# A recorded order and its PSUM banks, replaced from the third transposed load on, in an LN + long convolution + gated MLP backward kernel

## The chip, the cores and the metric

The kernel runs on one core of a Trainium2 chip. The metric is the device time of one execution in microseconds (us). Before the change it is 425.65 us, the median of three runs (423.27 to 426.55).

## The reference, cut to what matters

The kernel returns the output and all nine gradients of a block on x of 2048 tokens by 512 channels, in bf16. With xn the layer norm of x:

```python
xn = _layernorm(x)
kv  = k_shift * v                                  # k_shift: 4-tap causal filter of k
y   = irfft(rfft(kv_pad) * rfft(ssm_k_pad))[:S] + kv * ssm_D
h   = (xn @ w_gate) * (xn @ w_up)                  # 1376 hidden channels
out = x + xn * y + h @ w_down
grads = vjp(out, (x, k, v, shift_k, ssm_k, ssm_D, w_gate, w_up, w_down))(grad_out)
```

The long convolution and its two gradients are done as Fourier transforms by matmul, in three stages that pass through DRAM.

## The kernel before, in words

Tokens are held as 16 rows r of 128 partitions. The work falls into four parts that overlap.

- A first part makes the layer norm, the hidden activations in six slices of the hidden width (mlp_rows, L416) and the weight gradients (dw_gen, L582). The hidden products go to the DRAM buffer HD.
- A second part (a_gen, s_gen) makes the first two stages of the Fourier transforms. Its result lies in the DRAM buffer CX.
- A turn (turn_gen, L615) transposes those slices of the hidden products that stay in SBUF: the last slice by TensorE in twelve groups of eight blocks with a ScalarE copy after each ("turn k", k being the first block), and rows 8 to 15 of the last but one by four transposing DMAs of two rows each ("turn load r").
- The last part is the one that the change touches. It runs over eight chunks n of two rows, rr = 0 and 1.

In the last part a chunk has these steps, named by their functions:

- **c_load(n)** (L676) brings 1.5 MB from CX into the one buffer C. It can be issued once the matmuls last_dft(n-1) have read C.
- **last_dft(n)** (L719), 24 small matmuls of 32 columns of weights into three two-bank PSUM slots; **c_dkv**, **c_y**, **c_o5** (L737, L729, L755) copy one slot each with ScalarE and go on with VectorE. c_o5 has one buffer and waits for its last store.
- **hd_load(n)** (L642) is a transposing DMA from HD into hdP[n % 2], 1152 rows of 768 for n up to 3 and 896 rows after. It can be issued once all matmuls of chunk n-2 have been done, and every matmul of chunk n waits for it.
- **y_o(n, rr)** (L784): 11 matmuls of 128x512 and a VectorE add into m[n % 2]; with rr = 1 the store of the output follows. **y_load(n)** (L688) refills m[n % 2] with x and so waits until the store of chunk n-2 has landed.
- **y_x(n, rr)** (L801): 22 matmuls of 128x512, then a VectorE and ScalarE chain for the gradient of x, with its store.
- **c_dsk(n)** (L764): VectorE products of the k gradient path and 8 small matmuls into one bank that is summed over all chunks; then **k_load** of the next rows.
- **dk_pair(r0)** (L710): seven VectorE operations into the one buffer dk, and its store. The next dk_pair begins by writing dk and so waits until the store has landed.
- **dkv_load** (L682) brings v and the shifted k for the next chunk.

All DMAs are issued by SyncE (SP) in one order, so an issue that waits holds all later ones. The functions above only record operations (class Eng, L143). emit (L181) decodes the string PLAN (L34): first a permutation of the 2271 recorded operations (a run of up to four matmuls is one), then a bank for each of the 398 PSUM slots. Each engine, and SP as the DMA queue, issues its operations in that order:

```python
    def emit(plan):
        raw = zlib.decompress(base64.b85decode(plan))
        order = struct.unpack(f"<{len(ops)}H", raw[:2 * len(ops)])
        for s, b in zip(slots, raw[2 * len(ops):], strict=True):
            s.base = Q[b // 2] if s.n == 2 else halves[b]
        ...
            for i in order:
                for fn in ops[i].fns:
                    fn()
```

A slot of two banks lies at an even bank ("F2" is banks 2 and 3, "h7" is bank 7). All instructions of the record carry line 173 in the profile (the line that calls the recorded function), so they are told apart by operation, shape, tiles and place in the order. big is the one SBUF tile, PP the one PSUM tile.

Of the kernel before, what the change touches and what calls it, by code (L numbers as in the profile page):

```python
# [17 lines left out]
S = 2048  # L18
D = 512
F = 1376  # L20
R = 16
# [9 lines left out]
RING = 28  # L31
RO = [0, 16, 24, 40, 56, 72]
EPS = 1e-5
PLAN = "c-l=@V-Ti0&yLfzZQHhO+qP}nwr$(CjpN;8V{!03yYHWGn(4G@t|V9PnWi^DCP)GdB_IW)gkq2Y1hPO$h!2S&As{4&;-FyQ5FiRfg=kO;qC*TQ4ap!Tl!aK32+BZv=m_N?HpGEk5Esfr1xN)OAs*z0`H%-TK?mprogp>khXT+7TEPNH3V9(76of9&8nQwmC=B^vEOdkJPy}j2S7-)Bp(Qkjy3hmaKu@R#)nF*hfcj7cszU>)3hAH`41<}_7%D*<m<Z#cG7N@>Fa&DAIA{XBpdw6z;V=Sf!eN*WXJ8fVf~GJE_P|J(0IOjVjE3FN7WzS2*bBX31>}S=FblF^R@?{sVK%IUBXAEAV;?vRN$?<4$D~*T=fWJA2g&dN9D;0E6W2h0SPOlj7G}qvU^1+O^{^NQz<c=-mcT&R01IIeY=zBm3${UeI0rw&QuqZjz!t~|7vN8bj>}*>{0iq`3S5L8a2&G13AhiJAO{|W-{2ZNf@AO)lH*B8fu|rP{th|uGNi)WkQ)Dh>mc|8d<tnWE#80!a1+wuT}Y3)Fau`9hmZ;Hz;nn9neip$#?RmrsEv70F)tdvfb8%uI06Q&gLM%xAGU*fSRda&evE<zupl<Tzn~%h2Zit|d=7;%DmKE#_!gc*5p06%uqm#`4Y(2CK?~f3e?v=bg{`p-ehJO+J+#H0unlA2XdHu2;45f{(Qq@i#}3#WzkrSy6Sv@DJc8pf7IwnU*af@d1nh=!@F+6Yg0JBf9K*lm8|aQ>@ik1w*q8&x;Xkk)dtwj#4!(t{I1MM_ah!v_a60zJt=I?WVqctsGq4{{!Uebk7vfAjfjjXe_QzQ`00-i39E4A42o1&+xC@71T%3o?a44?CB{&R+<5C<-gWwDn#rZe_pTTk*M$4fUjl_7k3K!#QY)y;sG&ZD!SPUCcacoQpFg~`S`ZS!@ViRghEvOmo!3J~+J5y6?NoTPOmB5*F9!uf{EQO`9BbC8(*oj6^J1UEpFcFr+D|j6VZ{STVkC*W(R=`_$8!O^$yn`cY6y3#2xR5I2J*<LN@gg>-`&bPh;6vPtG3fw4!pHaopJFU(PowY|&Z5{9hvL$6oJ}wAC0?R<^a*~7bLbH6$ItL{`~u@s0{RjYQX-m5U*SCJN2w?`<)Oi}4^vYbdWDJUHI||Nl$NexS(;B@<2P82^3pr$Kx61K<)iYHpDIu<DnQ@jclbSCfh3fU(o;psK$R#d{eVB>SjtG5=nDOW1?gwZOv$JaWudH8nSQ}v@i)vyzvCbHCuXO@l!N}l<Wz*J&>Or;Z?P!lq<7exM$<Jqi0|=l{0CFezxW>(qvBMRN)Qkd5mPl1nhI-B$;hcXrKCVLXaUuvC{&ViQB*2L(WoocqS{oNqEkJ(PK&7<-Jm+ugZj`CT1p#f8TF;^G>$gWc-leRXaG&1XEc$v(?D8Flju3^r1kWI*3o2oNgHSvZJ{YNjb_j-I!v2sDjlTLaD?{LCp4XQ(;@ni_Rs-3N-O9mI!1fxSGq|n={LGat7#Q2r=RH;Iz`{Z8Tyn?)93Vney6jvhEC99dPKs1&}a0JPSTSIN#%5$o|(U(44jc)Q6|pJU(uJ8g<n%v{)@KKZMsM2=nZA#?0lZ?P!7IJIr%;1;=d_3JAX~zQXU@4-_U*fj`A|__Y{|r<8chm$Hs4I7{8<8Je&We5j>Nl@xSs9jpTo%B9G#j9G^#XbdJJfxByS*Nt}SA@(iB9u{btY;>tXW=kP?X!U@^5AQ$4vJdUe!(0$|zI-V18Vvc+wox(}DFjwOr=szjKMVWOfFX8IEh>CGiu1hgURCN(Y(PX@olXG-U!O?U9AE)A6f=hB#jj0QHF~`t2nv!d9JnhVJwG^k)RGgYib9_ysHMtg-;aD15Q)?P7%jI|wrR4;gP|I^#t<4oUv8K~RnpE?19qz(Ov@X}<^qO4ja|X?*4LF&0<!;=aQ)mxv$UQlSX3|F7m~(0`PN{LYpf=&&+?1PfbIzp%V>!3B;8mPgm-AL`$(eN-=h3P<kGF9(ZN-IjF1O}B+=kooYVOO`HLGUVeq2;nayDJZS#%BO*Y&)X`*UHft@(5S7tuQUieGaHZO5gwJr~pBT2i-jUHzJOa2c(kwX`SI)Y4i`%j-by!1wt9SJ1NhkRS0NE})OOqITpbTuB@2V6LZC^eK1ZruvMZ^9%llo9IiftZlS`e#;y96K<rRa$Eh38|vr$1-H{?`W=7CEwsIM((m~PuCG7xPuxM1NK%=`1GKqz)MU~{f96)2TvA9k9i%Cxvu@;6GElo}FCC`cb-0euU7T9d$Ug3^Y2^U#=OLU<dg?DcSbyb%oL>6s5N)Y@_&3fVLv=5Y)XjXDd*~MKqvLdf=8{94L;7h(>96B;y5^Kj(po2KZuy-v%VeFQJ2{(Vmn@P;{@`NrCr{GZT3lA^IbN%I<pQ1O3w)6;@fy9%qxA}xlB+yMgUr!c`X|lPO*~V_>Rdg}flJE*jUtOQs;tu!e3IwudL5-3G@2~Y5^{}K=tiBQQ#HDr;*zpVuk#I#Aq#btZqdbhhGWVmy~$-ImMquJdRTAqO8t+v>1|%YOZBM!#YcIE-r-|>m$&O1o~E&7kCu@`dXM+&TRzSEG>+tx8gfKy$q_!O`K6|u*4naD<H}jyrG@0U?$!blPfqADJ*9WFuAJ3^5?|hNVM!qOG@%rgM6#Rb^Lwr)iRG@I(VJRb_Uqq#OV8^;{f7@|Ik~OZ^k2TA5A?cj)gp3P&uMwNs{io?tt6MUf>f3(`cOeCN-KG!b>yOcu8*~uptP1J`h`B#``TQdX;t}3TSx<GBvquPJlAjZGi@UcrLnx!PxZAvk{8-mKGE;=OT8yQXyl5MKlQP^(R%VqzvAEIFTF1h<ZBiANgv9$s`6HUm-kv<x=B-cr{AkdJ8|hCPvu8#B7f^|`l~*Xj*?aW(SP-K{X@IUf7(Mj$yf5T{vp3;X90U9?S-tTd?C>dt(Ta6DbcLAxOI^}(pO^IGYQ7_iKso7xYkwrNq>o9VlO1V#j&XNsYJ1~_EH8&Jo{5#OFBz$f5|`@B!lH^86vT4sHC!C65A43LOUaAEUC?uvvN)n*?CEA87#3Sw+nJnl2}HYC6^?b&6YWm$x_;9lG!fH6?tNFC52s;d6M6<SXRqs1#P}$w*_)d7Rq&5Bsp!dd}{fuu;s8^_LJO@&!wp4wgQ&Nc1vDcBHzhyd1}S2r2QZx<gwk9TT;YE%2HV-Kg(@-BYUK*6|+LNTvkYF`%y~RD!C(N?75ASQdZ8&+h|!WE9HBsYGY)tRI`fqneCJPQr*VN8d)n9?0_7Ub+TS+*aq1swQQV>mv7{d)U@L^K{iP{dt~3rMA<Brtg=m#$<p4YNEPc~Q)QZLk&af^4$BcaDz&YXb++kJ$GX@I`Bl1FJzHdp?S*ZXZL(dC$xHj!y4i8rA>Hj4>0$Nlnf0^=c0x`{FI!>_ZKo`?M)p>A$th`UO>Cl_mZsL*`dBk-ZhftVwX{~&&sy6uTW)P^lC`xJw$dis=QhQ@u)8wVR@pTB!KT{``_g`~&GyRr+W`CBw%Att(FWRTTVvboHydPwZLQ6;A$H1!+ICxK!)(3Hve~x7hT9xFXLIdm`@}Zb2-|7%Y?tk}pX@7pZF_8_&9{wq-WJ$i`_A^+e*42l*#R4E3+;OwW2fy`8*2w`oV~G4Hr~FmLpH(Q+F|?Jj#wH`>+kFzOX|VXd2zpC;_oert4H^!9>dAmGkOU(kLe{nmM8X07R~>*GZx!3`Av)Cf13McJ8S8^fXDUBp2Z9LQOoM_9KDDq@oZk%<NFmW<$u{d%kDWnhhMPPe$}dbX|LfmJ%y+AGM>O|`L~we?^_%1;JLh`7xHBOpJnjeUf64UCok)ry{$L)I)2d-dO6SIO+At4^}3$V>v=IR?-jg>SM(~L+LL=x@8Vs3npg66KHa<d4DaFHeWthfYTnNqcz++}seFLX@=5-{s`_vr;oytBnGg1rzRm~wI3MZty`lH?UcSml`4aEzjeLmr_VqsAS9>3C?hoyn-Lla>##{Mqo9!EXj!*D;-ooel8sF$+eWGvj&HmE2_)wqhEq$wBw<*5YkNPLR&$s!fzSyVwXMWI+_!qv`zx4Tj!MFPkf8fV_sek2Xe1X66*M7y9`5-^;C;Y0P^*w&f7WyMU>F0cfFZZu~r|<StzRMr`A>Z%U{Iq}L=l!sM>(~9M-?8ughTrsCe%mklUH{zg+IJp8ln^yU3wQj9Kl4letKakA{Ib9GH~!qChZsS^4}RZ&@iZZAc<1Rt`j8=H3_p6z@ZSIQpZ$d&@Si+ZNFM(76d`3u6#nr{;a|@j;)JY00|X2de)lASgNMZ7q5tKvLzWOf#0{y!f1WT{C>RQbilI`d9IAw5p=ziWs)r__X=oO5hom81XdYUIY$1Cn8w!USp-8A1YK2yzb!ZdXhIS!O$RBcr)Zv7c45dQpFg6qo#lpBSK1>J`!=%t4)D8_p@sK0@;W<P5Ff=3xB|^tgC)5pPLb=c(<PGIRg-|~f2z^7pFgbJzox`v&Jgg5>!idl!^bd`~v@kVH4?RMcFd%dfGs3{IA#4nrLeH={YzeEv>d+?)3UfoZFgVN(2gBAdG7Jf$!b#f}Mu!FAT38bnhCN|>=o%V_d|^je6c&e_VOLlZ#)PGzUYHqrg=JxFI1~<tBjIQ`7LJFL;Y64hmWNZ}e7GKNgqz`3xE*?j-C<U^6V8P>;X*ha_J)1oZnzlMg~#DZxF61hOW|3#7xsq(;cR#w9)ySCQFsxahL_=TxDu|0`C&y^8PE(h@>&OuJdRl$1;jkkvV<cGV|8b9VK<TwVnPB$=nz2yut(mg&XMg$eMBOYdBh(YlUv05M-35tfJ5X*$`HYcBVaU&C?X9sf-;G`&P7?#6h1WY$Tkuk6e5=hY9yRS%$N)#Ds+K}wMDu%LL?;vwFo$}h-kr3JOch8Zi*52{~HmZj}bp4Y4nlM2Ra`~StP}X(Z~6t0YQWk{QvPm_rKFf&L8>OM>ig+AJB)$fRQq?=m$!X)FMY8YUPm}<U`K<p+XTV5iq!abdUbQB*N3>1I_;fuWN+;"  # L34
KB = 1024


# [1 line left out]
def kernel(  # L39
# [141 lines left out]
# [5 lines that stand above are left out]
        with tc.manual_schedule(engines={mybir.EngineType.PE, mybir.EngineType.DVE, mybir.EngineType.Activation, mybir.EngineType.Pool, mybir.EngineType.SP}):  # L186
# [3 lines that stand above are left out]
# [452 lines left out]
    def hd_load(n):  # L642
        a, b = hd_span(n)
        ldT(out=hdP[n % 2][:, :, 0:b - a], in_=HP[n, a:b])
# [292 lines left out]
    for n in range(NCH):  # L937
# [32 lines left out]
        else:  # L970
# [4 lines left out]
            if n + 2 < NCH:  # L975
                y_load(n + 2)
                hd_load(n + 2)
    emit(PLAN)

# [106 lines left out]
```

## Time and profile before

| | |
|---|---|
| Median of three runs | 425.65 us (423.27 to 426.55) |
| The profiled execution, its own time | 425.49 us |
| Its span (first to last instruction) | 423.7 us |
| Busy: TensorE / VectorE / ScalarE | 409.3 / 348.6 / 261.2 us |
| The DMA queue | 126.75 MB, 95.1% of 16 engines' span |
| Granted TensorE clock over the span | 0.998 |

The profiled execution's own time is 1.8 us more than its span. The page gives sums over the span; the last part of the kernel lies between about 285 and 423 us, and the views that bear on it are the timelines of TensorE, VectorE and SP there, the waits, and the chain that ended last. Because each run of the recorded operations keeps its order, the instructions of a timeline can be matched one by one with the decoded PLAN: by weight loads on TensorE (all 3190 are in the trace), and by instructions on VectorE, ScalarE and SP. Times of named operations below come from that matching.

### The profile page before, as it was taken

How to read it: one execution, taken by the hardware profiler on the slowest of the kernel's cores; microseconds unless marked ns; L12 is line 12 of the kernel's file. 1: busy time of each engine (PE TensorE's matmuls, PEld its weight loads, DVE VectorE, ACT ScalarE, POOL GpSimd, SP SyncE). 2: the span in 40 equal slices, each digit the busy share in tenths (PEclk: the TensorE clock that was granted, in tenths of full speed). 3: DMA queues.
4: the chain of work that ended last, by engine and by line, in shares of the span. 5: the costliest groups of instructions: out<-in, count | busy, mean ns of one | idle time of the engine just before them, and what ended most of it. 6: DMA issues, size and time to landing. Idle time of an engine off the chain costs nothing.

```text
span 423.7 us, 8079 instructions
## 1 busy us (share of the span) xinstructions
PE 409.3 (97%) x3135; PEld 199.1 (47%) x3190; DVE 348.6 (82%) x653; ACT 261.2 (62%) x380; POOL 3.5 (1%) x9
## 2 busy tenths in 40 slices
PE   8999999999999999999999999999999798999996
PEld 5745555754454333544444434444544343444443
DVE  5999969998659999899999980325858697999996
ACT  4856988598545999898999953363515333242323
POOL 1000000000000000000000000000000000000000
PEclk9999999999999999999999999999999999999999
DMA  8989999999797878969789999999999999999974
GB/s 307 398 198 372 317 320 383 347 367 348 271 347 258 325 263 320 309 231 342 278 295 352 302 312 307 314 349 248 221 306 302 270 261 303 305 326 296 266 216 164
DMA packets 104367, 127.27 MB, mean 300 GB/s; under 512 B 63877, under 2 KB 74250, under 8 KB 103305
## 3 DMA queue, kind: packets, MB, share of 16 engines
q1 hardware_dynamic: 104328, 126.75, 95.1%
q8 instruction: 25, 0.41, 0.4%
q14 instruction: 14, 0.11, 0.1%
HBM read 57.10 MB, written 54.04 MB: 262 GB/s over the span
## 4 chain that ended last, share of the span: by engine, by line
PE 81%; DVE 8%; DMA 5%; SPq 2%; issue 1%; ACT 1%; ACTq 0%; DVEq 0%
PE PP L173 81%; DVE big L173 8%; DMA big<-CX 4%; SPq L173 2%; ACT big L173 1%; DMA out_dram<-big 1%; DMA big<-in_x_dram 1%; ACTq L173 0%; DVEq L173 0%
## 5 line engine op out<-in xcount | busy, mean ns | idle before, releaser
L173 PE MATMUL PP<-big 128*128 128x512 bf16 (+8 forms) x3135 | 409.3, 350 | 10.5 <-DMA big<-CX 4.0
L173 DVE TENSOR_TENSOR big<-big 128x1024 bf16<-128x1024 bf16 (+2 forms) x465 | 267.5, 631 | 46.9 <-ACT big L173 36.1
L173 PEld LDWEIGHTS <-big 128*128 128x128 bf16 (+3 forms) x3190 | 199.1, 97 | 220.2 <-issue 57.7
L173 ACT CAST big<-PP 128x512 bf16<-128x512 f32 (+2 forms) x314 | 224.2, 781 | 86.5 <-PE PP L173 66.7
L173 ACT ACTIVATE big<-big 128x1 f32<-128x1 f32 (+3 forms) x46 | 23.6, 522 | 47.9 <-DVE big L173 45.5
L173 DVE CAST big<-PP 128x512 bf16<-128x512 f32 (+1 forms) x37 | 32.4, 875 | 9.6 <-PE PP L173 5.0
L173 ACT COPY big<-PP 128x1024 bf16<-128x1024 bf16 x15 | 14.9, 1010 | 20.6 <-PE PP L173 20.6
L173 DVE SCALAR_TENSOR_TENSOR big<-big 128x512 bf16<-128x512 f32 (+2 forms) x36 | 23.1, 653 | 0.2
L173 DVE SCALAR_TENSOR_TENSOR big<-big,PP 128x512 f32<-128x512 bf16 x14 | 9.6, 684 | 9.0 <-PE PP L173 8.9
L173 DVE BATCH_NORM_STATS2 big<-big 128x6 f32<-128x512 bf16 x16 | 10.5, 681 | 2.8 <-DMA big<-in_x_dram 2.8
L173 DVE TENSOR_TENSOR big<-big,PP 128x512 bf16<-128x512 bf16 x14 | 9.3, 683 | 1.3 <-PE PP L173 1.3
L173 POOL MEMSET big<- 128x1536 bf16 (+2 forms) x3 | 2.9, 950 | 250.9 <-PE PP L173 250.9
L173 DVE TENSOR_SCALAR big<-big 128x512 bf16<-128x512 bf16 (+1 forms) x13 | 4.6, 385 | 0.0
L173 ACT ACTIVATE big<-PP 128x512 f32<-128x512 f32 x2 | 1.2, 597 | 3.5 <-PE PP L173 3.5
L173 DVE BATCH_NORM_AGGREGATE big<-big 128x2 f32<-128x6 f32 x16 | 2.3, 167 | 0.1
L173 DVE RECIPROCAL big<-big 128x2 f32<-128x2 f32 (+1 forms) x9 | 1.2, 149 | 0.7 <-ACT big L173 0.7
L173 ACT ACT_TABLE_LOAD x1 | 1.3, 1283 | 0.7 <-PEq L1074 0.7
L173 DVE DVE_READ_ACCUMULATOR big<-big 128x1 f32 x16 | 1.3, 82 | 0.0
L173 DVE DVE_READ_ACCUMULATOR big<-big,PP 128x1 f32 x14 | 1.2, 83 | 0.0
L173 DVE MEMSET big<- 128x128 bf16 (+1 forms) x2 | 0.2, 112 | 0.8 <-PEq L1074 0.8
L173 DVE COPY big<-PP 128x1024 bf16<-128x1024 bf16 x1 | 0.7, 692 | 0.2 <-PE PP L173 0.2
L173 ACT ACTIVATION_READ_ACCUMULATOR big<-PP 128x1 f32 x2 | 0.4, 194 | 0.0
(6 smaller groups left out, 0.9 us busy)
## 6 DMA issues: line engine op xcount, KB each, us to landing
HD<-big SPq DMA_DIRECT2D x32, 384.0 KB, 5.6
AX<-big SPq DMA_DIRECT2D x16, 768.0 KB, 5.4
big<-AX SPq DMA_DIRECT2D x16, 768.0 KB, 6.2
CX<-big SPq DMA_DIRECT2D x16, 768.0 KB, 5.1
out_dram<-big SPq DMA_DIRECT2D x43, 256.0 KB, 4.4
big<-CX SPq DMA_DIRECT2D x7, 1536.0 KB, 8.3
big<-in_vK_dram SPq DMA_DIRECT2D x8, 512.0 KB, 6.1
big<-in_w_dram SPq DMA_DIRECT2D x4, 768.0 KB, 7.5
```

Source lines behind the costliest of these rows:

```text
L173: o.fns.append(lambda: f(*[fix(x) for x in a], **{kk: fix(x) for kk, x in k.items()}))
```

## The change

Only the string PLAN changes:

```diff
-PLAN = "c-l=@V-Ti0&yLfzZQHhO+qP}nwr$(C...
+PLAN = "c-l=@V-O}wua47e+qP}nwr$(CZQHhO8...
```

No operation is added or removed. Decoded, the two orders agree up to the 858th of TensorE's 1009 entries, the 446th of VectorE's 623, the 312th of ScalarE's 377 and the 180th of SP's 259. From there 109, 154, 48 and 63 places hold another operation. 39 of the 398 PSUM slots lie in other banks, all of them in this last part. POOL's order is the same.

SP's order, from the first difference to the first third of what follows ("=" marks the same place):

```
place  before                        after
180    hd_load(1)                    store out, chunk 0
181    shift of dks, chunk 1         hd_load(1)
182    = store o5, chunk 1
183    shift of dks, chunk 0         c_load(3)
184    hd_load(2)                    store o5, chunk 2
185    shift of dks, chunk 1         dkv_load(3), v
186    store out, chunk 0            store dk_pair(0)
187    store dv, chunk 2             y_load(2)
188    store dk_pair(0)              store dv, chunk 2
189    c_load(3)                     hd_load(2)
...
195    dkv_load(3), v                store out, chunk 1
196    store out, chunk 1            c_load(4)
197    hd_load(3)                    k_load
198    shift of dks, chunk 1         shift of dks, chunk 1
199    c_load(4)                     hd_load(3)
```

The large issues and what stands between them further on:

```
before: 207 store out(2) .. 209 hd_load(4), 210 turn load 8, 211 c_load(5), 213 y_load(4),
        218 store out(3), 219 hd_load(5), 220 y_load(5), 227 c_load(6), 229 hd_load(6),
        230 store out(4), 231 turn load 12, 234 y_load(6), 237 c_load(7), 239 store out(5),
        240 hd_load(7), 241 y_load(7), 242 store dk_pair(10), 243 turn load 14
after:  204 turn load 8, 206 hd_load(4), 207 store out(2), 209 y_load(4), 210 to 217 eight small
        ones, 218 c_load(5), 219 hd_load(5), 220 store out(3), 221 and 222 two stores,
        223 y_load(5), 224 c_load(6), 230 store out(4), 231 hd_load(6), 233 turn load 12,
        234 y_load(6), 237 c_load(7), 238 store out(5), 240 hd_load(7), 241 y_load(7),
        242 turn load 14, 243 store dk_pair(10)
```

TensorE's order around last_dft (mm is a matmul of 128x512):

```
before: dft(2), 14 mm y_x(0,1), turn 40, dsk(0), turn 80, turn 24, chunk 1 (66 mm),
        16 mm of y_x(2,0), dft(3), dsk(1), ... chunk 2 and three turns ..., 4 mm of y_o(3,1), dsk(2),
        dft(4), ... chunk 3, dsk(3), one turn ..., 16 mm of y_x(4,0), dft(5), dsk(4), ...
after:  dft(2), dsk(0), 14 mm y_x(0,1), chunk 1 (66 mm) with turns 64, 24, 72, 80 in it, dft(3),
        dsk(1), chunk 2 (66 mm) with turns 48, 40 and dsk(2) in it, dft(4), dsk(3), chunk 3 (66 mm),
        turn 88 and 44 mm y_x(4,0), y_x(4,1), dft(5), dsk(4), ...
```

On VectorE the changes are swaps within a chunk for the most part: in the after order the products of c_dsk(1) stand ahead of y_x(0,1), and the store's last add of y_o(5,0) stands at place 579 rather than 569. From the last dft on, TensorE's order is the same but for dsk(6), behind dft(7) rather than ahead of it, dsk(7), ahead of the last two halves of y_o(7,1) rather than behind them, the order of these halves, and the place of three matmuls.

2 lines of the change are left out of this document (1 added, 1 removed).

## The prediction

> **What bounds the kernel now.** I read the busy shares first, then the last part alone, because everything up to 295 us keeps its order.
>
> ```profile
> PE 409.3 (97%) x3135; PEld 199.1 (47%) x3190; DVE 348.6 (82%) x653; ACT 261.2 (62%) x380; POOL 3.5 (1%) x9
> ...
> q1 hardware_dynamic: 104328, 126.75, 95.1%
> ```
>
> TensorE is nearly full, and so is the DMA queue. What an order can win is TensorE's idle time in the last part. The timeline of TensorE shows it:
>
> ```profile
> 336.91 1.48 PE L173 MATMUL PP<-big 128*32 128x512 bf16 x24 [2.08 <-DMA big<-CX]
> ...
> 358.08 2.26 PE L173 MATMUL PP<-big 128*32 128x512 bf16 x32 [1.65 <-DMA big<-CX]
> ```
>
> These are dft(4) and dft(5), each waiting for its c_load. With 0.27 at dft(7) and some pauses of 0.16 us the idle time after 295 us is 5.0 us: a floor under the gain, since no matmul goes away. Why the loads were late stands in the timeline of SP:
>
> ```profile
> 285.98 12.38 SPq L173 DMA_TRANSPOSE big<-HD  x1
> ...
> 300.93 7.15 SPq L173 DMA_TRANSPOSE big<-HD  x1
> ...
> 318.54 8.54 SPq L173 DMA_TRANSPOSE big<-HD  x1
> 327.13 2.45 SPq L173 DMA_DIRECT2D big<-big  x1
> 329.68 0.53 SPq L173 DMA_DIRECT2D big<-CX  x1
> ```
>
> A transposed load holds SP for 7 to 12 us, and c_load(4) came behind one (dft(3) had read C by 321). The chain of waits shows what sets the end:
>
> ```profile
> 329.68 7.19 DMA big<-CX
> ...
> 350.16 7.88 DMA big<-CX
> ...
> 401.07 3.51 DMA out_dram<-big
> 404.58 0.02 issue
> 404.60 2.57 DVE big L173 x4
> ```
>
> From 394.6 us on it is VectorE (hardly idle from 361), held at 404.6 by the landing of dk_pair(10)'s store, since dk is one buffer. So **both** TensorE's waits and VectorE's end must move for the time to fall.
>
> I take the new order with the durations of these rows: 0.216 us a matmul of 128x512 (four in 0.865), 0.53 a turn group, 1.9 to 2.0 a dft with its dsk, 0.45 a small issue on SP, 0.6 to 0.7 a VectorE operation (0.42 the 512-wide ones, 0.9 to 1.2 the wide ones).
>
> **1. hd_load(1) behind the output store.** The store needs VectorE's add that ended at 291.66; with its issue hd_load(1) starts at 292.3, not 285.98. Before, its packets could not run earlier anyway: other loads landed until 294.4. hd_load(2), alone in the queue, landed 9.25 us after its issue (300.93 to 310.18), so hd_load(1) lands at 301.55. TensorE asks for it earlier than before, since three turns go to a later place: 295.05 + 1.9 (dft(2), dsk(0)) + 14 x 0.216 = 299.97. **A new stall of 1.6 us.** Bounds: 0.3 if it lands in 8.0 (1.4 to the first packet, 6.1 at rate, 0.5 to the semaphore), 5.3 if it takes hd_load(3)'s 13.0 (the slowest of 1152 rows). I take 1.6, the row with an equally empty queue. The rate is this row of the windows (last column GB/s, the one before it the DMA share):
>
> ```profile
> 304.00:309.00 5.00, 5.00 (x25) 2.24 (x23) 3.69 (x7) 3.34 (x4) 0.00 (x0) 1.00 1.27 290
> ```
>
> 1152 x 768 x 2 bytes at 290 GB/s are 6.1 us. The Trainium skill ("DMA: Bandwidth & Descriptors", section "Latency and other measured facts") gives 261 GB/s for a transposing DMA; by that the load would take an estimated 6.8 us, the stall would be 2.3 and the sum 425.7. The trace's 290 decides.
>
> **2. dft(3), dft(4), dft(5).** From 301.55 to dft(5) TensorE has 242 matmuls (52.3), seven turns (3.7), two dft with dsk and one dsk alone (4.6): dft(5) at 362.1. Before, dft(5) began at 358.08 with 28 matmuls (6.0) of chunk 4 still to do that now lie ahead of it, so the same work ended at 364.1: **2.0 us ahead**, if no load is late. The loads:
> - c_load(3) is issued at 300.6 (before 310.36), since it no longer stands behind hd_load(2). c_load(4): dft(3) has read C at 319.1, issue 319.1 (before 329.68), landing by 327, wanted at 335.5. The 2.08 goes.
> - hd_load(2) waits on SP behind the dv store of chunk 2 (VectorE 307.6): issue 308.1, not 300.93, landing 317.4 to 318, wanted at 319.7. hd_load(3): issue 322.9, landing 332 to 335, wanted at 337.4. Both are hidden, with 2 us to spare.
> - c_load(5) stands behind y_load(4), which waits for the landing of the store of out(2), which now stands right behind hd_load(4) in the queue (before, it was ahead). hd_load(4): issue 336.6, SP free at 343 to 345, landing 345 to 347, the store 347.5; nine issues of 0.45; c_load(5) at 351.8, landing 359.2, wanted at 362.1. The 1.65 goes, with 3 us to spare.
> - The same at c_load(6): y_load(5) waits for the store behind hd_load(5) (issue 354.8, landing 365): c_load(6) at 366.9, landing 373.5, wanted at 375.3.
>
> **3. Chunks 6 and 7: the lead is spent.** dft(6) starts at 375.3 (before 378.29). hd_load(6) waits on SP for VectorE's last add of y_o(4,1): issue 373.1, landing 382.3, wanted at 383.0. Turn load 12, behind it, lands at about 386.2 (386.00 before), wanted at 385.8: 0.5 of stall. c_load(7): 385.4, landing 394.0, wanted 393.9. hd_load(7) stands behind the store of out(5), whose last add now stands ten places later on VectorE and ends at 393.1 by the sum of its rows (with 1.1 of waiting for y_load(6)): issue 394.0, not 388.70. The queue is empty then, so it lands at about 402 (402.37 before). It is wanted at 401.7: 0.4 of stall.
>
> **4. The end.** Behind hd_load(7) come y_load(7), turn load 14 and only then dk_pair(10)'s store, which stood ahead of the turn load before. SP is free of hd_load(7) at 400 to 401.6, the turn load holds it 1.5 to 2.7, and the store lands at 405.1 to 406.7 (404.58 before). After that VectorE has 24 operations, 13.9 us (before 26 and 15.8). Its end: 419.0 to 420.6 against 420.42. TensorE would be through at 419.4 against 419.76. The last store follows in either case.
>
> **5. The banks.** The new slots ask for copies done earlier: y_o(1,1) in h0 needs c_dkv(2)'s copy (298.2 of 299.97), dft(3) in F2 the turn copies (315.9 of 317.7), dft(7) in F2 VectorE's add of y_o(6,0) (393.8 of 393.9). Costed at nothing; the last one has no slack, so what VectorE is late there TensorE is late too.
>
> **The sum.** Against its own 425.49: the ends are 1.4 earlier to 0.2 later, mean 0.6. 424.9, and as this execution lies 0.16 under the median, **425.0**. A gain of 4.0 in waits is answered by 1.6 at hd_load(1) and by the queue and VectorE at chunk 7.
>
> **The rivals.**
> - *The lead is kept (422.5).* hd_load(1) lands in 8.0 (stall 0.3) and VectorE, which follows TensorE, reaches the add of y_o(5,0) earlier, so hd_load(7) and the end move too: 425.0 - 1.3 - 1.2. For it: VectorE waited 9.2 us for TensorE in this part. Against it: from 361 us VectorE is itself full.
> - *SP is jammed behind y_load (431, between 428.5 and 433), the other side.* Place: y_load(4) and y_load(5), each waiting for a store queued behind a transposed load, with c_load next. If hd_load(4) takes 13.0 as hd_load(3) did, the store lands 2.2 after 349.6, c_load(5) is issued at 356.4 and lands 8.6 to 9.9 later, 365.0 to 366.3: a stall of 2.9 to 4.2. Then c_load(6) falls behind the later hd_load(5) and costs 1.9 to 2.8: 4.8 to 7.0 together. It decides from hd_load(4) landing after 348.5. For it: at 327 to 330 and 348 to 350 the packets of a transposed load stopped for a while. Against it: hd_load(2) and hd_load(5) landed 9.3 and 9.7 after their issue. The Trainium skill ("DMA: Bandwidth & Descriptors", "Queues, rings and completion order") says that each DMA engine takes descriptors in ring order, which is this rival's rule. The trace agrees: a shift issued at 308.14 landed at 310.46, after hd_load(2)'s 310.18.
> - *The order is not what sets the time (425.5).* The queue is 95% full, so the same bytes end at the same time. Against it: it was empty from 409 to 412.
>
> ```profile
> 409.00:412.00 3.00, 3.00 (x16) 1.36 (x14) 3.00 (x6) 2.00 (x4) 0.00 (x0) 1.00 0.00 0
> ```
>
> **How the numbers follow.** Forecast (423.2 to 427.5) 0.48; lead kept 0.16, of which 0.10 below 421.4; jam 0.33, of which 0.30 above 429.9; order without effect 0.03. One per cent, 4.3 us, is about what a measurement of this kernel can tell from no change. Faster 0.10, same 0.60, slower 0.30. The range, 421.5 to 432.0, leaves out a tenth on each side.
>
> **What would show it.** TensorE's timeline: a gap of about 1.6 us in front of y_o(1,1) near 300, none before dft(4) and dft(5). SP: c_load(4) near 319, c_load(5) near 352, hd_load(7) near 394. The chain's last part: VectorE behind dk_pair(10)'s store, landing at 405 to 407. It is wrong if a transposed load takes much more or less than 9 us, or if VectorE waits where I gave it none.

## The result and the profile after

The changed kernel takes **430.12 us** (median of six runs, 429.44 to 432.92) where the kernel before takes 425.86 in the same comparison. The comparison's estimate of the ratio is 1.0133, with a 95% interval of 1.0098 to 1.0169; the quotient of the two medians alone is 1.0100. The forecast was 425.0, a little faster than before, and the kernel is slower. The time lies inside the range, where one of the rivals had put it (SP jammed behind y_load, 431), and 2.6 us outside the forecast's own part of it (423.2 to 427.5).

The profiled execution took 431.25 us, with a span of 429.5. It is 1.1 us behind the profiled execution of before at dft(2) already (296.14 against 295.05), up to where both orders are the same; that much of any later difference is not the change's.

The page of after, busy shares, the queue's row, and the group of all matmuls with the idle time ahead of them:

```profile
PE 410.3 (96%) x3133; PEld 199.1 (46%) x3190; DVE 350.8 (82%) x653; ACT 261.2 (61%) x380; POOL 3.5 (1%) x9
...
q1 hardware_dynamic: 104328, 126.75, 92.7%
...
L173 PE MATMUL PP<-big 128*128 128x512 bf16 (+8 forms) x3133 | 410.3, 352 | 13.7 <-DMA big<-CX 4.5
```

The bytes are the same, the queue's share of the longer span is 92.7% instead of 95.1, and 4.5 us of TensorE's idle time wait for a load from CX. VectorE is 2.2 us busier with the same 653 instructions; that comes back below.

TensorE's timeline of after, start, length, and in brackets the idle time ahead and its releaser:

```profile
302.25 50.73 PE L173 MATMUL PP<-big 128*128 128x512 bf16 x314 [1.06 <-ACT big L173]
353.41 9.67 PE L173 MATMUL PP<-big 128*128 128x128 bf16 x49 [0.43 <-ACT big L173]
366.43 33.18 PE L173 MATMUL PP<-big 128*32 128x512 bf16 x189 [3.35 <-DMA big<-CX]
400.78 23.20 PE L173 MATMUL PP<-big 128*32 128x512 bf16 x145 [1.17 <-DMA big<-CX]
```

The waits of before at dft(4) (2.08) and dft(5) (1.65) were to go. The first went: 50.73 us without a gap lie across dft(4) at 336.12. The second has become 3.35, and dft(7) waits 1.17 instead of 0.27. The 1.06 at 302.25 is the new stall of step 1. The releaser named there is ScalarE, but hd_load(1) landed at 302.20, 0.05 ahead of the start.

SP's timeline of after, start and time that SP was held:

```profile
321.70 0.37 SPq L173 DMA_DIRECT2D big<-CX  x1
...
324.12 11.59 SPq L173 DMA_TRANSPOSE big<-HD  x1
...
340.88 6.79 SPq L173 DMA_TRANSPOSE big<-HD  x1
347.72 1.91 SPq L173 DMA_DIRECT2D out_dram<-big  x2
351.69 0.34 SPq L173 DMA_DIRECT2D big<-in_x_dram  x1
...
354.45 1.85 SPq L173 DMA_DIRECT2D out_dram<-big  x3
356.77 0.33 SPq L173 DMA_DIRECT2D big<-CX  x1
```

These are c_load(4), hd_load(3), hd_load(4), the stores of out(2) and o5(3), y_load(4), the last small stores and c_load(5). hd_load(3) holds SP for 11.59 us behind c_load(4). hd_load(4) starts 4.3 us later than forecast. From 349.6 to 351.7 SP stands for y_load(4), which waits for the landing of out(2)'s store (351.63). Eight more small issues take it to 356.77.

The chain that ended last, of after, its last part:

```profile
356.77 9.62 DMA big<-CX
...
391.33 9.40 DMA big<-CX
...
407.79 3.46 DMA out_dram<-big
...
416.79 3.01 DMA out_dram<-big
419.82 5.38 DVE big L173 x10
```

c_load(5) and c_load(7) are on it, and then the stores of dk_pair(10) and dk_pair(12), each of which VectorE waits for (0.39 and 0.83).

Windows of after: length, busy times, granted TensorE clock, DMA share, GB/s.

```profile
331.00:356.00 25.00, 24.41 (x145) 10.83 (x141) 23.15 (x45) 9.54 (x14) 0.00 (x0) 1.00 1.08 229
351.00:357.00 6.00, 5.57 (x32) 2.69 (x32) 5.17 (x11) 3.73 (x5) 0.00 (x0) 1.00 0.73 214
365.80:369.20 3.40, 2.77 (x28) 1.09 (x32) 3.40 (x8) 0.77 (x3) 0.00 (x0) 0.51 1.19 266
```

And one window of before, which begins as far behind its dft(2):

```profile
330.00:355.00 25.00, 22.61 (x139) 10.02 (x140) 21.86 (x41) 7.61 (x12) 0.00 (x0) 1.00 1.13 290
```

In these 25 us the queue of after carries 229 GB/s where before carries 290: 61 x 25 are 1.5 MB less, as much as one c_load. And for 3.4 us after the wait at dft(5) the granted clock is 0.51; dft(5) takes 2.74 us instead of 1.47, so the wait costs another 1.3.

### The profile page after: what moved, and what is told of

The parts are those of the page before. It is cut to its first block, busy times and chain, and to the rows that moved or that the text cites. A ratio compares the mean times of both kernels' runs of the same rounds, so it can differ in the third digit from the quotient of the medians.

```text
span 429.5 us, 8079 instructions
## 1 busy us (share of the span) xinstructions
PE 410.3 (96%) x3133; PEld 199.1 (46%) x3190; DVE 350.8 (82%) x653; ACT 261.2 (61%) x380; POOL 3.5 (1%) x9
## 3 DMA queue, kind: packets, MB, share of 16 engines
q1 hardware_dynamic: 104328, 126.75, 92.7%
## 4 chain that ended last, share of the span: by engine, by line
PE 74%; DVE 10%; DMA 9%; SPq 2%; issue 2%; ACT 1%; DVEq 0%; ACTq 0%
PE PP L173 74%; DVE big L173 10%; DMA big<-CX 4%; DMA out_dram<-big 2%; SPq L173 2%; ACT big L173 1%; DMA big<-in_w_dram 1%; DMA big<-big 1%; DVEq L1082 0%; DVEq L173 0%; ACTq L173 0%
## 5 line engine op out<-in xcount | busy, mean ns | idle before, releaser
L173 DVE TENSOR_TENSOR big<-big 128x1024 bf16<-128x1024 bf16 (+3 forms) x465 | 269.4, 633 | 48.4 <-ACT big L173 35.8
```

The lines of the kernel that those rows point to most:

```text
L173: o.fns.append(lambda: f(*[fix(x) for x in a], **{kk: fix(x) for kk, x in k.items()}))
```

## The experiments

All kernels keep the operations of both kernels. They change only the recorded order, but for the last two (e17, e18), which keep the order and shorten one load. Ratios are the estimate against the kernel before, run in the same comparison, with its 95% interval; after has 1.0133. A holder, below, is whatever by its own lateness keeps an operation from starting; an operation can have several at once.

### One issue of SP moved

If the jam behind hd_load(4) is a single wait, moving one issue past it should free c_load(5). Three kernels do that on the after order. Edits of SP's order:

```diff
 e1_y4:                  e2_c5:                   e3_hd1:
 store o5(3)             hd_load(4)              -store out(0)
-y_load(4)              +c_load(5)                hd_load(1)
 8 small issues          2 stores, y_load(4)     +store out(0)
 c_load(5)               8 small issues
+y_load(4)              -c_load(5)
```

> The changed order with one issue moved: y_load(4) behind c_load(5) instead of behind the store of chunk 2. Theory J (SP is held by y_load(4), which waits for a store that lies behind hd_load(4), and c_load(5) comes late): in the changed kernel SP stood 2.1 us there, so c_load(5) is issued 2 us earlier or more (354.5, not 356.8), dft(5) waits 1 to 1.5 instead of 3.35, time 427 to 428. Theory O (the same jam has a second holder: the store of o5 of chunk 4 waits for a ScalarE copy, which waits for the store of o5 of chunk 3, also behind hd_load(4)): SP stands there instead, c_load(5) at about 355.7, gain 1 us at most, time 429. Theory V (the end is set by VectorE and later chunks, whatever dft(5) waits): no change, 430.

Measured: 437.83, ratio 1.0286 (1.0220 to 1.0351). VectorE's timeline shows who pays:

```profile
367.54 2.75 DVE L173 TENSOR_TENSOR big<-big 128x1024 bf16<-128x1024 bf16 x4 [10.04 <-DMA big<-in_x_dram]
```

c_y(4) waits 10 us for y_load(4), which is now behind c_load(5). dft(5) then waits 8.46 us, and its releaser is VectorE. None of the three theories came: c_load(5) is issued at 357.89, no earlier than in after, since SP no longer stands for y_load(4) but goes on standing for the stores of dk_pair(4) and o5(4) behind it.

> The changed order with one issue moved: c_load(5) directly behind hd_load(4), ahead of the store of chunk 2, y_load(4) and eight small issues. Theories J and O both: c_load(5) is issued at about 348 (not 356.8), lands by 355, dft(5) is wanted at 363 and does not wait; the gap of 3.35 us goes and with it the half clock behind it: time 425.5 to 427. Theory V: the wait moves on to chunks 6 and 7 and the time stays at 429 to 430.

Measured: 436.80, ratio 1.0268 (1.0207 to 1.0329). dft(5) has no gap. But the store o5(3), now behind c_load(5), lands at 359.10, and ScalarE's copy of c_o5(4) waits for it:

```profile
359.18 1.01 ACT L173 CAST big<-PP 128x1024 bf16<-128x1024 f32 x1 [8.40 <-DMA out_dram<-big]
```

With its bank not read, TensorE waits 5.74 at turn 88. The store of out(2) is late in the same way, and SP stands from 351.7 to 358.7 for y_load(4).

> The changed order with one issue moved: hd_load(1) ahead of the store of chunk 0. The stall in front of y_o(1,1), 1.06 us in the profile, should go. If everything behind it follows TensorE: 429. If the later waits are set by SP's own order (theory J): less than 0.5 is left of it, 429.7 to 430.

Measured: 430.31, ratio 1.0139 (1.0057 to 1.0221). The stall of step 1 is gone, and the time stays. In its place TensorE waits 0.67 for hd_load(2) and 0.95 for hd_load(3), and dft(5) still waits 2.86. The lead has no value while the loads come when they do.

The whole of SP's order of before, under the engine orders and banks of after:

```diff
-SP: order of after from place 180
+SP: order of before from place 180
```

> The changed orders of TensorE, VectorE and ScalarE and the changed banks, with the order of SP from the kernel before. Theory J/O (the loss lies in SP's order): 424 to 426.5, as before. If the loss lies in the engines' orders or the banks: 429 to 431.

Measured: 443.47, ratio 1.0427 (1.0366 to 1.0488), the slowest of all. SP stands from 359.9 to 372.5 for a dkv_load whose buffer VectorE frees later in its new order. SP's order and the engine orders are a pair, and neither can be judged alone. (The other half, SP's order of after under the engine orders of before, was not run.)

### Repairing the place behind hd_load(4)

In after o5(3) is ready at 321.2 and out(2) at 332.6, and both are stored only behind hd_load(4), from 347.7 on. e5 moves the first store ahead of it, e6 both; e8 shortens hd_load(3) instead; e7 builds the same arrangement into the before order.

```diff
 e5 / e6 (after):        e7 (before):             e8 (after):
+store out(2)           -store o5(3)             -c_load(4)
+store o5(3)   (e6)     -store out(2)             2 small issues
 hd_load(4)              hd_load(4)               hd_load(3)
-store out(2)           +store out(2)            +c_load(4)
-store o5(3)   (e6)     +store o5(3)
 y_load(4)              +y_load(4)
                         turn load 8, c_load(5)
```

> The after order with one issue of SP moved: the store of out(2) ahead of hd_load(4). Several holders (my theory): y_load(4) no longer waits for this store, but the store o5(3) still stands behind hd_load(4), lands near 352, so the ScalarE copy of c_o5(4) still starts at 352.3, the store that follows it at 354.5 and c_load(5) at 356 to 357. dft(5) still waits 3 us; the time stays that of after, 429 to 431. One holder (rival): the wait of y_load(4) for the landing, 2.1 us of SP, is what makes c_load(5) late; then c_load(5) is issued at 354.5, dft(5) waits about 1 us and the time is 426 to 428. Order without effect: as after.

Measured: 429.97, ratio 1.0105 (1.0061 to 1.0149); c_load(5) at 355.91. Neither the time nor the load has moved by as much as 1 us, as several holders said.

> The after order with two issues of SP moved: the stores of out(2) and of o5(3), both of results done by 331, ahead of hd_load(4); y_load(4) then stands directly behind hd_load(4). Several holders (my theory): hd_load(4) is issued 2 us later (342.5), SP is free at 349.3, y_load(4) follows at once, the copy of c_o5(4) starts near 348.7, the last wait left is that of the store of dk_pair(4) for VectorE (351.9), c_load(5) is issued at 353.5 to 354.5 and lands by 362 to 364; dft(5), wanted at 363.0, waits 0 to 1 us, turn 88 not at all, the clock stays near 1. Of the 430.1 of after go 3 to 3.8 of waits and up to 1.3 of clock: 425 to 427.5. VectorE as the end (rival): TensorE's waits go, but VectorE ends where it ended, and the time is 429 to 431. Order without effect: 429 to 431.

Measured: 430.85, ratio 1.0116 (1.0068 to 1.0164). My theory said 425 to 427.5. SP's timeline of e6:

```profile
342.38 8.22 SPq L173 DMA_TRANSPOSE big<-HD  x1
350.70 0.53 SPq L173 DMA_DIRECT2D big<-in_x_dram  x1
...
353.71 1.91 SPq L173 DMA_DIRECT2D out_dram<-big  x3
355.73 1.08 SPq L173 DMA_DIRECT2D big<-CX  x1
```

y_load(4) stands right behind hd_load(4) without a wait, and c_load(5) is still issued at 355.73, only 1.0 us earlier than in after: hd_load(4) begins 1.5 later behind the two stores and holds SP for 1.4 longer, and behind it y_load(4) and eight small issues take 5.0 us by themselves. dft(5) waits only 0.95 all the same, as my theory had it, and the clock stays at 1.00; yet the time is that of after. So the stall at dft(5) is not by itself what the time hangs on.

> The before order (engines, banks and SP) with three issues of SP moved: the stores of out(2) and o5(3) and y_load(4), in this order, directly behind hd_load(4), that is, the arrangement of after in the order of before. Several holders (my theory): SP is free of hd_load(4) near 346, the stores land at 349 to 351, y_load(4) is issued then, turn load 8 holds 2.7 and c_load(5) is issued at 353 to 355 (350.16 in before), landing 361 to 363: dft(5) waits 4.5 to 6.5 instead of 1.65, or TensorE waits for the copy of c_o5(4) instead. 428 to 431 (before 425.5). Rival, the jam needs the rest of the new order: c_load(5) goes back by less than 1 us, and the time is 425 to 426.5.

Measured: 427.57, ratio 1.0059 (1.0025 to 1.0093), between my theory and the rival. The same arrangement does not make the jam in the order of before: only turn load 8 stands between it and c_load(5), which is issued at 349.61, no later than in before (350.16), and dft(5) waits 1.86 (1.65). What costs the 0.6% is not shown.

> The after order with one issue of SP moved: c_load(4) directly behind hd_load(3), not three places ahead of it. The transposed load is long because c_load(4) is ahead of it in the queue (my theory): hd_load(3), issued near 322, holds SP 7 to 9 us instead of 11.6 and lands 9 to 10 after its issue instead of 13.6, near 331.5; c_load(4) is issued near 330 and dft(4) waits about 2 us, as in before; hd_load(4) is issued at 336 to 338 instead of 340.9, and c_load(5) comes 3 to 4 us earlier than in after, so that dft(5) waits 0 to 1 instead of 3.35. Time 427 to 430. Rival, a transposed load of this size takes 12 to 14 us at this place whatever lies ahead: hd_load(4) is issued at 340 or later, both waits stand, and the time is 431.5 to 433.

Measured: 430.60, ratio 1.0122 (1.0065 to 1.0178), just above the range of my theory. SP's timeline of e8:

```profile
324.10 8.25 SPq L173 DMA_TRANSPOSE big<-HD  x1
332.45 0.52 SPq L173 DMA_DIRECT2D big<-CX  x1
...
336.10 3.92 SPq L173 DMA_TRANSPOSE big<-big  x1
340.06 0.60 SPq L173 DMA_DIRECT2D out_dram<-big  x1
340.78 6.20 SPq L173 DMA_TRANSPOSE big<-HD  x1
```

hd_load(3) holds SP 8.25 us instead of 11.59, so the c_load ahead of it was what made it long. But turn load 8, now closer behind c_load(4), takes 3.92 instead of 1.69, and hd_load(4) starts where it did. My step from a shorter hd_load(3) to an earlier hd_load(4) was wrong. c_load(4), now issued at 332.45, makes dft(4) wait 3.31.

### VectorE's neighbours

From dft(2) on VectorE has the same 179 operations in both kernels. Its end, counted from dft(2), is 130.12 - 125.37 = 4.75 us later in after. Of that 1.7 are waits (19.26 in all against 17.55). The other 3.0 are the distances from start to start where nothing waits. Matching each instruction with its operation shows why: a 1024-wide operation takes 0.60 us to the next start, but 0.72 if the next one reads its result or, as in some of the pairs, writes over what it has read. Before has 16 such neighbours in this part, after 39, and 23 x 0.12 are 2.8 us. e9 sets them apart in after, e10 makes as many in before, e12 takes away those of before.

```diff
 e9, e12: VectorE            e10: VectorE
 x                           x
+w (inputs there already)   +y
 y, reads x                  w
-w                          -y, reads x
```

> The after order with SP's, TensorE's and ScalarE's orders and the banks untouched; 25 operations of VectorE are moved ahead by 1 to 6 places, only where their inputs had been there in after's trace, so that an operation that reads the result of the one right ahead of it gets another one in between. Of such neighbours after has 39 in the last part (17 from 359 us on) and before has 16 (6); after these moves 14 are left (9). Theory that neighbours cost time: an operation followed by a reader of its result takes 0.72 us to the next start, else 0.60, in both traces. The busy time of VectorE falls by 25 x 0.12 = 3.0 us; 1.0 of it lies behind 359 us where VectorE is hardly idle and comes off the end in full, of the rest a part is swallowed by waits: 427.5 to 429.3. Rival, the end is set by SP's queue alone (dft(5)'s wait and the stores of dk_pair): VectorE's time falls but its waits grow by as much: 429.5 to 431.

Measured: 431.62, ratio 1.0132 (1.0087 to 1.0176). VectorE's work falls by 2.5 us (its end less its waits), its waits grow by 1.9, and the time stays. The longer busy time is real and was covered.

> The before order with SP's, TensorE's and ScalarE's orders and the banks untouched; 20 operations of VectorE each change places with the one ahead of them, so that 39 operations of the last part, as in after, read the result of their neighbour (16 in before). Neighbours cost time: VectorE's busy time grows by 23 x 0.12 = 2.8 us; some two thirds of it lie behind 359 us: the time grows by 1.5 to 2.8, to 427 to 428.5, and nothing else of the profile changes much. Rival, VectorE's own time is covered by the queue's waits: 425 to 426.3.

Measured: 425.89, ratio 1.0018 (0.9981 to 1.0055). The work grows by 2.9 us and the waits fall by 2.4; my 1.5 to 2.8 did not come.

> The before order with ten operations of VectorE moved ahead by 1 to 5 places in the same way as in the after order with neighbours apart: 6 neighbours left of 16 (4 of 6 from 359 us on). Neighbours cost time: 0.2 off the end for sure, up to 1.2 in all: 424.4 to 425.6 where before gives 425.6. Rival, no effect or a wait in place of it: 425.4 to 427.

Measured: 423.97, ratio 0.9979 (0.9943 to 1.0015): the lowest ratio of a kernel that leaves nothing out, but not told apart from before. No version was found that beats both kernels for certain.

### Everything together

```diff
 e11, SP's order of after:
+store out(2), store o5(3)
 hd_load(4)
 y_load(4)
+store y_x(2,1), store dk_pair(4), c_load(5)
 6 small issues (2 k_loads, 2 loads of v and ks, 2 stores)
 ...
 turn load 12
+c_load(7)
 y_load(6), 2 stores
 ...
+store dk_pair(10)
 turn load 14
 (and VectorE's neighbours apart)
```

> The after order with what the runs so far point to, all together: the stores of out(2) and o5(3) ahead of hd_load(4); y_load(4) directly behind it, then the stores of y_x(2,1) and dk_pair(4), then c_load(5) with the six small issues behind it; c_load(7) directly behind turn load 12; dk_pair(10)'s store ahead of turn load 14; and VectorE's neighbours set apart (11 left of 39). Theory of several holders and neighbours together: c_load(5) is issued at 352.5 to 353.5, dft(5) does not wait, dft(7) does not wait, VectorE needs 3 us less; of after's 430.1 go 0.9 (dft(5), on top of what the two stores gave), 0.8 (dft(7)), 2 to 3 (VectorE) and 1 to 2 of the stores: 424 to 427. Rival, a further holder takes their place (hd_load(5) earlier and in the way of the dk store, a late load of v or k): 428 to 431.

Measured: 436.69, ratio 1.0251 (1.0204 to 1.0297): the rival by its mechanism, and worse than its 428 to 431. VectorE waits 4.79 for a k_load and 5.98 for y_load(6): both had been put behind a c_load and landed with it, 8 us later.

### Where the loss arises

At the places where both orders have the same operations left, the front of one can be joined to the end of the other.

```diff
 e13: after  up to SP's c_load(7), TensorE's y_x(6,1)  +  before from there
 e14: before up to there                               +  after  from there
```

> The after order up to the 978th of TensorE's entries (y_x(6,1)), the 582nd of VectorE's, the 358th of ScalarE's and the 238th of SP's (c_load(7), out(5)'s store), the before order from there on, where both orders have the same operations left; each part has its own banks. Loss in the middle and in the end (my theory): by dft(7) after's TensorE lies 3 us behind in the two traces and after TensorE's end another 1.5 us are lost; with the end of before the 1.5 go: 428 to 429.3. Rival, the end only follows: as after, 429.5 to 431. Rival, the end is most of it: 425.5 to 427.

Measured: 432.33, ratio 1.0181 (1.0136 to 1.0226), above all three ranges. The end of before behind the front of after gives nothing back.

> The other way round: the before order up to the same places, the after order from there on. Loss in the middle and in the end (my theory): before's time and 1 to 1.5 us: 426 to 427.3. Rival, the end only follows: as before, 424.5 to 425.8. Rival, the end is most of it: 428 to 430.

Measured: 425.44 where before gave 423.78, ratio 1.0040 (1.0008 to 1.0073). TensorE's timeline of e14:

```profile
284.63 51.36 PE L173 MATMUL PP<-big 128*128 128x512 bf16 x341
336.27 80.56 PE L173 MATMUL PP<-big 128*32 128x512 bf16 x486 [0.28 <-DMA big<-CX]
```

By e13 the front of after brings as much loss as the whole of it. By e14 its end on a quick front costs between 0.1% and 0.7%, 1.7 us by the medians, as my theory for that run had it; behind the slow front this does not show. So most of the loss, not all of it for certain, arises ahead of 400 us. The window of e14 from 331 to 356 carries 323 GB/s:

```profile
331.00:356.00 25.00, 24.72 (x155) 10.69 (x157) 23.92 (x44) 7.92 (x13) 0.00 (x0) 1.00 1.11 323
```

### Two and three repairs at once, and the disputed load by itself

```diff
 e15: SP as in e6, VectorE as in e11 (e9's order with 11 neighbours left, not 14)
 e16: e15, and behind y_load(4):
+k_load, store y_x(2,1), store dk_pair(4), c_load(5)
 5 small issues
-c_load(5)
```

> The after order with two repairs that have been run one by one: the stores of out(2) and o5(3) ahead of hd_load(4), and VectorE's neighbours set apart (11 left of 39), nothing else. Both are needed together (my theory): with the stores early VectorE has less to wait for after 355 us, so that its 3 us of saved time come off the end: 427 to 428.8. Rival, something third holds the end, the queue that has carried too little by 360 us: 429.5 to 431.5.

Measured: 428.83, ratio 1.0101 (1.0058 to 1.0144). The median lies 0.03 above the range of my theory, but before was quick in this comparison too (423.78), and the ratio's interval overlaps that of after: no gain is shown.

> The two repairs of the run before (stores ahead of hd_load(4), VectorE's neighbours apart) and a third: c_load(5) stands behind y_load(4), one k_load and the stores of y_x(2,1) and dk_pair(4), ahead of the five issues that can wait. The queue's hole is the rest (my theory): c_load(5) is issued near 353 and lands near 361.5, dft(5) does not wait (1.19 before this step), the queue carries 0.6 to 1 MB more by 60 us behind dft(2), and the time falls by 1 to 2 us to 426.5 to 428. Rival, what is put behind c_load(5) is late instead (8 us): VectorE waits for it and the time is 429 to 432.

Measured: 431.63, ratio 1.0169 (1.0124 to 1.0214). dft(5) does not wait, as said. TensorE's timeline of e16 shows what does:

```profile
372.24 7.20 PE L173 MATMUL PP<-big 128*128 128x512 bf16 x37 [1.20 <-DMA big<-HD]
379.78 7.84 PE L173 MATMUL PP<-big 128*32 128x512 bf16 x52 [0.35 <-DMA big<-CX]
389.52 18.02 PE L173 MATMUL PP<-big 128*128 128x512 bf16 x103 [1.90 <-DMA big<-HD]
```

hd_load(5) and hd_load(6), each behind a c_load in the queue, are late now, and VectorE waits 3.86 at dk_pair(8).

```diff
 e17 (after), e18 (before), in c_load:
-            ld(c[p], src[p])
+            q = (4 * 3 * D) // (4 if n == 5 else 1)
+            ld(c[p, 0:q], src[p, 0:q])
```

> The after kernel, in which c_load(5) brings only the first quarter of its 1.5 MB; dft(5) reads old data for the rest, so a part of the input of chunk 5's transforms is left out. All other instructions and orders stay. The lateness of c_load(5) is the loss (my theory): it lands near 361.5, dft(5) does not wait, the clock does not fall, hd_load(5) comes 3 to 4 us earlier: 424 to 426.5. Rival, the loss lies in more places: dft(5)'s wait goes, but the time falls by 2 or less, to 428 to 430.

Measured: 429.04, ratio 1.0104 (1.0055 to 1.0153). c_load(5) lands at 363.59, and dft(5) still starts only at 366.00. TensorE's timeline of e17:

```profile
366.00 0.40 PE L173 MATMUL PP<-big 128*32 128x512 bf16 x4 [2.17 <-DVE big L173]
```

The releaser is VectorE. VectorE's timeline of after shows what it is doing there:

```profile
359.23 2.14 DVE L173 TENSOR_TENSOR big<-big 128x1024 bf16<-128x1024 bf16 x3 [2.96 <-DMA out_dram<-big]
362.25 1.03 DVE L173 TENSOR_TENSOR big<-big 128x1024 bf16<-128x1024 bf16 x2 [0.88 <-DMA out_dram<-big]
...
364.87 1.28 DVE L173 TENSOR_TENSOR big<-big,PP 128x512 bf16<-128x512 bf16 x2
```

The last row is the adds of y_o(3,1) and y_o(3,0), which read banks 4 and 5. dft(5)'s first slot lies there in after (in banks 0 and 1 before), so it cannot start before 365.6 in bank 4 nor go on in bank 5 before 366.15, whatever the load does. The last matmuls of the two had ended at 356.2 and 354.7. Their adds come 9 to 11 us later, behind operations that wait: VectorE stands for the stores of dk_pair(4) (2.96) and of y_x(2,1) (0.88), both issued after 353 by SP. In after the load landed at 366.39: **two holders less than 1 us apart**, and the wait is put down to the later one. In e17 the same two adds end at 365.94 and 366.54, and dft(5) starts at 366.00 and goes on at 366.60.

> The same in the before kernel, c_load(5) with the first quarter of its bytes, the rest of its data left out. My theory: before loses 0.3 to 1.65 us at dft(5); the time falls by 0.5 to 2.5: 422 to 424.5, so that the two orders are 1 to 3 us apart instead of 4.5 to 5. Rival, the loss lies in more places: before gains as much as after and the distance stays at 4 to 6 us.

Measured: 423.90, ratio 0.9969 (0.9939 to 0.9999). Before gains about as much as after, and the distance stays at 5.1 us: the rival, the loss lies in more places than this load.

## Why the prediction was wrong

**Step 1 held.** The new stall is 1.06 us (forecast 1.6, between 0.3 and 5.3); hd_load(1) took 9.0 us to land (9.25). e3 shows that it was worth nothing to the end.

**Step 2 failed at hd_load(4) and c_load(5).** Up to dft(4) its result held: c_load(4) was issued at 321.70 (forecast 319.1), and the 2.08 is gone. Then hd_load(3) was to land at 332 to 335 and landed at 337.73: it was issued 1.2 late (324.12 for 322.9) and held SP for 11.59 us. Of the rows I had, I used 9 to 12 us to its landing, those of loads with no large load just ahead. The new order puts c_load(4) three places ahead of it, and hd_load(1) and hd_load(7) of before, each right behind a c_load, had held SP for 12.38 and 11.58; e8 shows that this is what made it long. hd_load(4) was so issued at 340.88 instead of 336.6, c_load(5) at 356.77 instead of 351.8, and it took 9.6 us to land instead of 7.4. The 3 us to spare became 3.35 of stall. That is the term that went wrong in the forecast; it is not all of the loss, since with the stall at 0.95 (e6) or gone (e16) the time does not come back. The step also counted on the TensorE waits of before as a property of its order. In the four other profiles whose front is that of before or close to it (e7, e10, e12, e14) the wait at dft(4) is 0.2 to 1.0 and at dft(5) 0 to 1.9, where the one that I had read shows 2.08 and 1.65; in e14, where the front is the same to the last operation, they are 0.28 and none. So much of the gain that I booked was not the order's to give. (The 5.0 us of idle time that I called a floor under the gain are an upper limit to it.)

**Step 3** has everything 5.7 to 5.9 us late from hd_load(6) on (378.88 for 373.1, c_load(7) 391.33 for 385.4, hd_load(7) 399.71 for 394.0): that is what dft(5) left behind, the 1.1 of the whole profile among it. Only the wait at dft(7), 1.17, is larger than was given there. c_load(6) did not stall.

**Step 4**: after the landing of dk_pair(10)'s store VectorE took 15.0 us (forecast 13.9): 0.83 of it is the wait for dk_pair(12)'s store, of which I had given none. The store landed at 411.25, not at 405 to 407, and most of that is the late front (e13); what the end costs by itself lies between 0.1% and 0.7% (e14).

**Step 5 failed.** The banks were costed at nothing, and of the slots with little slack I named three. dft(5) in banks 4 and 5 was not among them, and it is the second holder at the place where the stall is. No run moves this bank alone, so its price by itself is open.

**The jam rival** had the place, and nearly the numbers: c_load(5) at 356.4, landing by 366.3, 2.9 to 4.2 of stall, against 356.77, 366.39 and 3.35. It had the cause half right. The condition, hd_load(4) landing after 348.5, was met because it was issued late, not because it took 13 us: SP was free of it after 6.79, and TensorE read it from 351.08 on. c_load(6), which was to cost 1.9 to 2.8, cost nothing; the clock and dft(7) took that place in the sum. And the jam is not a single cause: with the wait behind y_load gone (e5, e6) the time stays. So the nearness of its 431 to the 430.12 is in part luck.

**The sum** by the two traces, from dft(2) to the end of the span: 133.4 against 128.7 us. TensorE's end is 3.1 later: its listed waits are 2.0 more (6.0 against 4.0), and 1.3 are the lower clock. VectorE ends 1.6 later still, and the last stores as long after it as in before.

**What stays open.** The runs show that most of the loss arises ahead of 400 us and that none of the waits moved here holds it alone. The queue's lower rate over these 25 us fits it (229 to 255 GB/s in after, e3, e6, e13, e15, e16 and e17, 290 to 325 in before, e12 and e14), but e8 carries 288 GB/s there and is no quicker, because it pays at dft(4) instead (3.31). I argue, and have not shown, that the root is the distance of 30 us between dft(4) and dft(5) on TensorE (21 in before): C is one buffer, so only one c_load can be made in these 30 us, and then hd_load(5), c_load(6) and hd_load(6) have to follow one another closely. TensorE's order alone was not tried.

## What to carry to other kernels

A queue that takes issues in order has a price list by position: what stands behind a large load lands with it, here 8 us later, and a transposed load behind it holds its issuer half as long again, so each moved load has to be costed with what is ahead of it in its new place. A wait with one releaser in the profile may have a second one less than a microsecond earlier (a bank, a store, the issuing itself), so before a wait is booked as a gain, look up when its other inputs were there. And idle time that one profile shows may belong to that execution and not to the order; read it in a second execution before spending it.

## What the runs showed of the hardware

- **A transposed load behind a c_load.** Over the 20 traces (140 loads from HD), one with a c_load issued up to 3.6 us ahead of it held SP for 9.5 to 13.1 us (39 loads; 8.2 behind the quartered one), one with the last c_load more than 5 us ahead 5.3 to 9.3; the seven in between 7.4 to 11.3.
- **VectorE's neighbours**, 0.72 instead of 0.60 us to the next start where that one reads the result or writes over an input, on the operations of 1024 columns and those of y_x's chain alike. The Trainium skill ("VectorE: DVE Perf Modes", section "The DRAIN you can't avoid") says that eight copies with a semaphore after each took as long as with one after the last. These traces differ: here an operation whose reader follows takes 0.12 longer, and the measurement decides.
- **The clock.** After waits of TensorE of 2.75, 2.85, 3.31 and 3.35 us (e13, e9, e8, after) the granted clock fell to 0.5 for some 3.4 us; after 2.17 and 2.08 (e17, before) it stayed at 1.00, and also after 2.86 in e3. The Trainium skill ("TensorE: Matmul & The Clock Gate", section "Part 1: The HAM clock gate (the "warmup" mystery)") puts this down to a free-running window of about 3.4 us, which would explain why 2.86 passed and 2.75 did not. The length agrees (in after it fell at 365.8 and rose at 369.3), and so does the free running: in each of the 20 traces the changes of the clock lie whole multiples of 3.41 us apart (58.03, 17 of them, from the rise to the next fall in after). That a whole idle window of that length is needed does not: it fell 2.7 us into a wait that had begun at 363.1. With windows laid on these multiples, it fell at the end of the nine that held 2.09 us of idle TensorE or more (e9 the least), and of none that held 1.90 or less (e16 the most); e3's 2.86 is split into 1.13 and 1.73.
